# Attention and SwiGLU FFN on one core: joined score stretches, block-diagonal tails, and X^T of batches 1 to 7 by DMA transpose

## The chip, the cores and the metric

The kernel runs on one core of a Trainium2 chip. The metric is device time of one execution in microseconds; before the change it was 412.75 us (median of 3 runs, 411.9 to 414.39). Engine names below: PE is TensorE (matmul), PEld its weight loads, DVE VectorE, ACT ScalarE, POOL GpSimd, SP the engine that here only issues DMAs. Tile names in the profile lines: QKT (QK in the first two batches) the transposed Q and K, `st` or `s` the score tiles, PT their exponentials, VN the values of V, `X` or `f` the banks that value sums go to, XN the attention output, XS the same after normalizing, XT its transpose; WG, WV and WO are the FFN's gate, value and down weights, th and HT the steps between its up and down projections (HT also takes the first loads of q and k), ob the output.

## The reference

```python
# q, k, v: 8 batches, 8 heads, 576 positions, 64 wide
scores = q @ k.T / 8
mask   = (pos_i // 64) >= (pos_j // 64)          # blockwise causal
attn   = softmax(where(mask, scores, -1e9))
x      = (attn @ v)                               # 4608 tokens x 512
xn     = x / sqrt(mean(x*x) + 1e-6) * rms_g
out    = (silu(xn @ w_gate) * (xn @ w_val)) @ w_out    # 512 -> 1536 -> 512
```

## The kernel before

It works pair of heads by pair of heads ("slots", four per batch, 32 in all and four more at the end). A slot holds the score matmuls, exponentials and value matmuls of the attention; between these pieces a budgeted number of FFN steps from a queue is put in, four matmuls of 512 columns each, so that PE has work while ACT and DVE do the softmax. Matmuls write to PSUM, which the kernel divides into eight banks of 512 fp32 columns: two for scores, two for values, four for the FFN. It writes a bank again when the bank's last reader is done. The FFN of a batch can begin when its normalized X has been transposed ("X^T"). The parts that matter here:

```python
ST = ps.tile([P, 2 * BANK], FP32, name="st")                        # 2 PSUM banks: scores
XB = [ps.tile([P, BANK], FP32, name=f"X{i}") for i in range(2)]     # 2: values (and tails)
FB = [ps.tile([P, BANK], FP32, name=f"f{i}") for i in range(4)]     # 4: FFN, in rotation

def qk(self, dst, h, c, lo, w):              # head h: partitions 64h to 64h+63
    ds = slice(h * D, (h + 1) * D)
    mm(dst, KT[ds, k0:k0 + P], QT[ds, lo:lo + w])       # 64 rows, two heads side by side

# scores(n): the group's matmuls into ST, then one exponential of 1024 columns ST -> PT.
# In group 2 also the last 64 keys ("tail"), one matmul and one exponential per head,
# into the last 64 columns of XB[0] and XB[1]:
    self.qk(XB[h][:, BANK - BLK:BANK], h, NC, TAIL, BLK)
...
# norm_scale: XS = X / rms (bf16).  norm_transpose: per 128 columns, PE transposes into an
# FFN bank, ACT copies to X^T with the norm weight as per-partition scale.
    pe(nc.tensor.transpose(x[:, j*P:(j+1)*P], XS[:, j, p*P:(p+1)*P], ident))
    nc.scalar.activation(out=xt_tiles[i][:, p, ...], in_=x[:, ...], func=AF.Copy,
                         scale=gscale[:, p:p + 1])
...
# a slot: scores 0, values 0 (of the previous pair), scores 1, values 1, scores 2,
# with a fifth of the FFN budget after each
```

The softmax here doesn't subtract the row's maximum and nothing guards it: scores larger than these inputs give would overflow.

## Time and profile before

| | before |
|---|---|
| time, median | 412.75 us |
| PE busy | 379.6 us, 92% |
| DVE busy | 249.4 us, 61% |
| ACT busy | 235.5 us, 57% |
| score tile waits (PE st <- ACT PT) | 7.4 us |

The first part of the page gives each engine's busy time, share of the span and number of instructions.

```profile
span 412.1 us, 7988 instructions
PE 379.6 (92%) x3096; PEld 193.4 (47%) x3096; DVE 249.4 (61%) x652; ACT 235.5 (57%) x451; POOL 134.0 (33%) x184
```

Where PE is idle is seen in the windows view (columns: window, its length, then busy time and number of instructions of PE, PEld, DVE, ACT and POOL; granted PE clock; DMA share; GB/s).

```profile
0.00:30.00 30.00, 14.40 (x187) 9.13 (x188) 15.55 (x59) 10.96 (x18) 20.01 (x31) 1.00 1.29 163
90.00:120.00 30.00, 27.79 (x231) 13.18 (x227) 18.80 (x46) 18.98 (x38) 14.86 (x20) 1.00 0.94 93
120.00:160.00 40.00, 39.60 (x326) 19.04 (x323) 27.00 (x71) 25.96 (x49) 16.85 (x24) 1.00 0.92 98
160.00:200.00 40.00, 39.67 (x325) 19.05 (x324) 26.19 (x72) 25.97 (x52) 16.85 (x24) 1.00 0.89 101
```

From 120 us on PE is busy 99% of the time, until its last matmul, and ACT and DVE have a third of their time free. There, only a shorter PE stream can shorten the kernel. What each piece of that stream costs is read from start to start, not from the recorded durations, because matmuls overlap. Two cuts of the PE timeline (start, length, operation, count):

```profile
135.36 0.44 PE L346 MATMUL f_90<-ident,XS 128*128 128x128 bf16 x5
135.64 1.03 PE L87 MATMUL f_91<-WO,HT 128*128 128x512 bf16 x4
...
143.38 1.03 PE L87 MATMUL f_88<-XT,WG 128*128 128x512 bf16 x4
144.34 0.39 PE L87 MATMUL st<-QKT 64*128 64x448 bf16 x4
144.67 1.04 PE L87 MATMUL f_89<-XT,WV 128*128 128x512 bf16 x4
145.54 0.61 PE L87 MATMUL X_87<-VN_95,PT_96 128*128 128x65 bf16 x15
```

Four matmuls of 512 columns take 0.87 us to the start of what follows (144.67 to 145.54). In front of a score stretch it is 0.96 (143.38 to 144.34), and the stretch itself takes 0.33 where its columns, two heads at a time, need 0.22: some 0.2 us per stretch go into entering and leaving. Five transposes of X take 0.28 us, 56 ns each, though each is recorded with more than 200 ns. The Trainium skill, "TensorE: Matmul & The Clock Gate", Part 1, gives 55 to 56 ns between matmuls of 128 columns at full clock; this trace agrees. (Its Part 4 gives about 275 ns for a PE transpose in a kernel; inside this busy stream that is nearer to the recorded length, 226 ns on average, than to the cost.)

The clock column needs one correction. The trace's record of the clock begins at 33.5 us, and the view prints 1.00 for the time that has no record. For most of that time PE ran at half speed: value matmuls start 55 ns apart up to 33.4 us and 29 ns apart from 33.6 us, and up-projection matmuls of 256 columns 213 ns up to 32.2 us and 109 ns from 33.7 us.

In the early part PE waits. The longest lines of the list of waits (who waited for whom: total us, times, longest):

```profile
PE f_88 L178 <- DMA HT<-in_q_dram: 6.5, 2, 4.7
PE st L87 <- ACT PT_96 L246: 4.0, 5, 1.6
PE X_87 L87 <- DVE XN L284: 3.3, 4, 2.1
PE f_91 L87 <- ACT ob L408: 2.1, 6, 0.5
PE st L87 <- ACT PT_96 L249: 1.8, 2, 1.0
PE st L87 <- ACT PT_97 L246: 1.6, 2, 1.0
...
PE X_86 L87 <- DVE XN L284: 1.0, 1, 1.0
```

The `st` lines are scores that wait until the exponential has emptied the one score tile (7.4 us together), the `X` lines are tails that wait until the values have left their bank (4.3 us).

### The profile page before, as it was taken

The numbers are of one execution on the slowest core, as the hardware profiler recorded it, in microseconds if no ns is written. First come the engines' busy times: TensorE is split into PE (matmuls) and PEld (weight loads), VectorE is DVE, ScalarE is ACT, GpSimd is POOL, SyncE is SP. The second block draws the span as 40 slices with busy tenths as digits, with TensorE's granted clock in tenths as the row PEclk, the third lists the DMA queues.
The fourth block names the chain that finished last, engine by engine and source line by source line (L and its number), as shares of the span: only waits on it lengthen the run. The fifth ranks groups of instructions, "written<-read, shape, count | busy, mean of one in ns | idle before, by whom it ended". The sixth has DMA issues, their size and how long they took to land.

```text
span 412.1 us, 7988 instructions
## 1 busy us (share of the span) xinstructions
PE 379.6 (92%) x3096; PEld 193.4 (47%) x3096; DVE 249.4 (61%) x652; ACT 235.5 (57%) x451; POOL 134.0 (33%) x184
## 2 busy tenths in 40 slices
PE   3469779887999999999999999999999999999996
PEld 2337545664444544454445444544454444444442
DVE  5455864673779276926692669267926872752760
ACT  2276756786585758576757575757674625322321
POOL 8643497886079006910691060000000000000000
PEclk9999998999999999999999999999999999999999
DMA  9999999999299639972998397231020002002002
GB/s 99 190 203 186 169 89 169 131 149 130 61 107 117 105 76 102 110 128 68 83 125 130 70 79 69 86 81 35 0 78 27 0 27 76 1 2 102 1 2 102
DMA packets 140950, 36.70 MB, mean 89 GB/s; under 512 B 127600, under 2 KB 136304, under 8 KB 140912
## 3 DMA queue, kind: packets, MB, share of 16 engines
q0 software_dynamic: 103712, 18.89, 56.8%
q1 hardware_dynamic: 37200, 17.31, 18.4%
q8 instruction: 24, 0.39, 0.4%
q14 instruction: 14, 0.11, 0.1%
HBM read 37.75 MB, written 9.44 MB: 115 GB/s over the span
## 4 chain that ended last, share of the span: by engine, by line
PE 75%; DVE 12%; ACT 7%; DMA 2%; issue 2%; POOL 1%; ACTq 0%; POOLq 0%; DVEq 0%
PE f_91 L87 19%; PE f_89 L87 15%; PE f_88 L87 15%; PE f_90 L87 12%; PE st L87 6%; PE X_86 L87 3%; PE X_87 L87 3%; DVE HT L395 2%; DVE th L389 2%; DVE XS L333 2%; DMA HT<-in_k_dram 2%; ACT th L388 2%; DVE XN L284 2%; ACT sq L318 2%; ACT PT_96 L246 1%
## 5 line engine op out<-in xcount | busy, mean ns | idle before, releaser
L87 PEld LDWEIGHTS <-WV 128*128 128x128 bf16 x480 | 43.5, 98 | 45.9 <-issue 6.9
L87 PEld LDWEIGHTS <-WG 128*128 128x128 bf16 x480 | 43.5, 98 | 42.9 <-issue 4.3
L87 PEld LDWEIGHTS <-HT 128*128 128x128 bf16 x432 | 38.6, 98 | 47.3 <-issue 9.6
L389 DVE SCALAR_TENSOR_TENSOR th<-th,f_88 128x512 f32<-128x512 f32 x53 | 36.4, 686 | 40.3 <-ACT th L388 39.9
L87 PE MATMUL f_90<-XT,WG 128*128 128x512 bf16 (+1 forms) x248 | 56.7, 356 | 0.0
L87 PE MATMUL f_91<-XT,WV 128*128 128x512 bf16 (+1 forms) x240 | 55.7, 358 | 0.0
L87 PE MATMUL f_89<-XT,WV 128*128 128x512 bf16 (+1 forms) x240 | 55.7, 358 | 0.0
L87 PE MATMUL f_88<-XT,WG 128*128 128x512 bf16 (+1 forms) x232 | 55.4, 366 | 0.0
L388 ACT ACTIVATE th<-f_88 128x512 f32<-128x512 f32 x53 | 31.9, 603 | 40.3 <-PE f_88 L87 39.2
L246 ACT ACTIVATE PT_96<-st 128x1024 bf16<-128x1024 f32 x44 | 45.1, 1024 | 16.2 <-PE st L87 16.2
L246 ACT ACTIVATE PT_97<-st 128x1024 bf16<-128x1024 f32 x44 | 45.7, 1038 | 11.4 <-PE X_87 L87 6.6
L87 PE MATMUL f_91<-WO,HT 128*128 128x512 bf16 x192 | 48.2, 384 | 2.1 <-ACT ob L408 2.1
L389 DVE SCALAR_TENSOR_TENSOR th<-th,f_90 128x512 f32<-128x512 f32 x55 | 37.7, 686 | 19.0 <-ACT th L388 18.9
L388 ACT ACTIVATE th<-f_90 128x512 f32<-128x512 f32 x55 | 33.1, 601 | 27.6 <-PE f_90 L87 24.6
L395 DVE TENSOR_TENSOR HT<-th,f_89 128x512 bf16<-128x512 f32 x54 | 37.1, 687 | 5.6 <-PE f_89 L87 1.6
L395 DVE TENSOR_TENSOR HT<-th,f_91 128x512 bf16<-128x512 f32 x54 | 37.1, 686 | 3.6
L78 POOL DMA_DIRECT2D VN_95<-in_v_dram x20 | 17.1, 874 | 51.6 <-PE X_87 L87 45.7
L87 PE MATMUL st<-QKT 64*128 64x512 bf16 (+4 forms) x240 | 28.2, 297 | 2.2 <-ACT PT_97 L246 1.6
L78 POOL DMA_DIRECT2D VN_94<-in_v_dram x20 | 17.1, 906 | 36.6 <-PE X_87 L87 36.6
L87 PE MATMUL f_88<-WO,HT 128*128 128x512 bf16 x108 | 26.2, 380 | 0.2 <-DVE HT L395 0.2
L78 POOL DMA_DIRECT2D QKN_92<-in_k_dram x30 | 23.0, 766 | 8.9 <-DMA QKT<-QKN_92 3.4
L318 ACT ACTIVATE sq<-XN 128x512 bf16<-128x512 f32 x40 | 25.6, 639 | 0.1
(126 smaller groups left out, 475.5 us busy)
## 6 DMA issues: line engine op xcount, KB each, us to landing
out_dram<-ob SPq DMA_DIRECT2D x36, 256.0 KB, 2.0
VN_94<-in_v_dram POOLq DMA_DIRECT2D x16, 128.0 KB, 4.8
VN_95<-in_v_dram POOLq DMA_DIRECT2D x16, 128.0 KB, 4.7
WG<-in_moe_w_gate_dram POOLq DMA_DIRECT2D x4, 384.0 KB, 10.8
WV<-in_moe_w_val_dram POOLq DMA_DIRECT2D x4, 384.0 KB, 11.7
WO<-in_moe_w_out_dram POOLq DMA_DIRECT2D x2, 768.0 KB, 14.0
QKN_92<-in_k_dram POOLq DMA_DIRECT2D x24, 64.0 KB, 3.5
QKN_92<-in_q_dram POOLq DMA_DIRECT2D x24, 64.0 KB, 3.6
```

The source lines that it names most:

```text
L78: return chain("POOL", nc.gpsimd.dma_start(**kw))
L87: pe(nc.tensor.matmul(dst, w, r, start=start, stop=stop))
L246: nc.scalar.activation(out=PT[:, a0:a0 + T4], in_=ST, func=AF.Exp, scale=SM_SCALE)
L284: nc.vector.tensor_tensor(out=xn_tiles[self.b][:, t0:t0 + n, f0:f0 + m * D].rearrange("p t (h d) -> p h t d", h=m), in0=xv[:, :, :, 0:D], ...
L318: nc.scalar.activation(out=sq, in_=XN[:, t, :], func=AF.Square, accum_out=ss[:, j:j + 1])
L333: nc.vector.tensor_scalar(out=XS[:, j, :], in0=XN[:, t, :], scalar1=rs[:, j:j + 1], scalar2=None, op0=ALU.mult)
L388: nc.scalar.activation(out=th, in_=pg, func=AF.Tanh, scale=0.5)
L389: nc.vector.scalar_tensor_tensor(out=th, in0=th, scalar=1.0, in1=pg, op0=ALU.add, op1=ALU.mult)
L395: nc.vector.tensor_tensor(out=ht, in0=gates.pop((i, k)), in1=pv, op=ALU.mult)
```

## The change

Three things at once. Score stretches: a second score tile, and two score groups one after the other, so that two slots have three stretches in place of six. Tails: the last 64 keys of both heads lie block-diagonally in one 128 x 128 K tile, so one 128-row matmul and one exponential do both heads. X^T of batches 1 to 7: root and norm weight are applied in one DVE operation, and DMA transposes issued from SP write X^T, with no PE transpose and no ACT copy. The second score tile takes the two X banks; values and tails now rotate through the four FFN banks.

```diff
-    ST = ps.tile([P, 2 * BANK], FP32, name="st")
-    XB = [ps.tile([P, BANK], FP32, name=f"X{i}") for i in range(2)]
+    ST = [ps.tile([P, T4], FP32, name=f"s{i}") for i in range(2)]
     FB = [ps.tile([P, BANK], FP32, name=f"f{i}") for i in range(4)]
+    def fbank(hold=None):                 # the oldest bank that no down sum holds
+        ...
+        def tail(self):
+            x = fbank()[:, 0:BLK]
+            mm(x, KT, QT[:, TAIL:S])      # KT block-diagonal: both heads, 128 rows
 ... norm_scale ...
+            nc.vector.scalar_tensor_tensor(out=XS[:, j, :], in0=XN[:, t, :],
+                                           scalar=rs[:, j:j + 1], in1=grow,
+                                           op0=ALU.mult, op1=ALU.mult)
+            ...   # for each FFN chunk that this tile touches
+                    sp(nc.sync.dma_start_transpose(out=xt(i)[:, :, lo - a:hi - a],
+                                                   in_=XS[lo - g0:hi - g0, j, :]))
 ... slots ...
-        at(norms, s1, lambda b=b, tiles=tiles: xt_by_pe(b, tiles))
+        if b == 0:
+            at(norms, s1, lambda b=b, tiles=tiles: xt_by_pe(b, tiles))
+        elif s % 2 == 0:
+            pieces = [lambda: session((cur, 0), (cur, 1))] + val + [None]
+        else:
+            pieces = [lambda: session((prev, 2), (cur, 0)), val[0],
+                      lambda: session((cur, 1), (cur, 2)), val[1], None]
 ... V and K tails loaded to match, PT cleared whole, norm weight row loaded at the start,
 ... one more QKT buffer, two more output buffers
```

More of the change, by code (lines that the diff above doesn't have):

```diff
@@ L47 @@
     TAIL = NC * P
-    PTW = 6 * BANK + 5 * BLK
+    T4 = 2 * BANK
+    PTT = 3 * T4
+    PTW = PTT + P + 3 * BLK
     const = ctx.enter_context(tc.tile_pool(name="const", bufs=1))
-    tp = ctx.enter_context(tc.tile_pool(name="tp", bufs=3))
+    tp = ctx.enter_context(tc.tile_pool(name="tp", bufs=4))
     xtp = ctx.enter_context(tc.tile_pool(name="xtp", bufs=3))
@@ L57 @@
     hbuf = ctx.enter_context(tc.tile_pool(name="hbuf", bufs=3))
-    obuf = ctx.enter_context(tc.tile_pool(name="obuf", bufs=2))
+    obuf = ctx.enter_context(tc.tile_pool(name="obuf", bufs=4))
     ps = ctx.enter_context(tc.tile_pool(name="ps", bufs=1, space=bass.MemoryType.PSUM))
@@ L87, in mm, with stbank @@
         pe(nc.tensor.matmul(dst, w, r, start=start, stop=stop))
-    ST = ps.tile([P, 2 * BANK], FP32, name="st")
-    XB = [ps.tile([P, BANK], FP32, name=f"X{i}") for i in range(2)]
+    ST = [ps.tile([P, T4], FP32, name=f"s{i}") for i in range(2)]
     FB = [ps.tile([P, BANK], FP32, name=f"f{i}") for i in range(4)]
+    held = set()
+    order = list(range(4))
     turn = [0]
-    def fbank():
+    def fbank(hold=None):
+        i = next(i for i in order if i not in held)
+        order.remove(i)
+        order.append(i)
+        if hold is not None:
+            held.add(i)
+            hold.append(i)
+        return FB[i]
+    def stbank():
         turn[0] += 1
-        return FB[(turn[0] - 1) % 4]
+        return ST[(turn[0] - 1) % 2]
     QKN = [const.tile([P, HP, 2 * NQT, P], BF16, name=f"QKN{i}") for i in range(2)]
@@ L100 @@
     PTS = [const.tile([P, PTW], BF16, name=f"PT{i}") for i in range(2)]
+    KB = const.tile([P, 2 * HP, P], BF16, name="KB")
     QK0 = [const.tile([P, 2, S], BF16, name=f"QK0{i}") for i in range(2 * HP)]
@@ L103 @@
     gscale = const.tile([P, HP], FP32, name="gscale")
+    grow = const.tile([P, DM], FP32, name="grow")
     WG = const.tile([P, HP, DFF], BF16, name="WG")
@@ L120, in load_v_tail @@
     def load_v_tail(b):
-        pool_dma(out=VN[b % 2][BLK:P, NC, :, 0:D],
-                            in_=v[b, :, TAIL:S, :].rearrange("h p d -> p h d"))
+        for par in range(2):
+            pool_dma(out=VN[b % 2][par * BLK:(par + 1) * BLK, NC, par:H:2, 0:D],
+                     in_=v[b, par:H:2, TAIL:S, :].rearrange("h p d -> p h d"))
     def load_v_chunk(b, c):
@@ L143, in load_qk_tail @@
             pool_dma(
-                out=t[0:BLK, :, NQT + NC, ds],
+                out=t[ds, :, NQT + NC, ds],
                 in_=k[b, par:H:2, TAIL:S, :].rearrange("h p d -> p h d"))
@@ L160, in clear_v @@
     def clear_v(i):
-        nc.vector.memset(VN[i][:, 0:NC, :, D:VP], 1.0)
-        nc.vector.memset(VN[i][0:BLK, NC, :, :], 0.0)
-        nc.vector.memset(VN[i][BLK:P, NC, :, D:VP], 1.0)
+        nc.vector.memset(VN[i][:, :, :, D:VP], 1.0)
+        for par in range(2):
+            nc.vector.memset(VN[i][(1 - par) * BLK:(2 - par) * BLK, NC, par:H:2, :], 0.0)
     def clear_qkn(i):
-        for n in range(2):
-            nc.vector.memset(QKN[i][BLK:P, :, n * NQT + NC, :], 0.0)
+        nc.vector.memset(QKN[i][BLK:P, :, NC, :], 0.0)
+        for par in range(2):
+            nc.vector.memset(QKN[i][par * BLK:(par + 1) * BLK, :, NQT + NC,
+                                    (1 - par) * BLK:(2 - par) * BLK], 0.0)
     tposed = {}
@@ L182, in tpose_wide @@
                                   in_=t[:, 0:S].rearrange("p (s j) -> p j s", s=SLOT))
-        tposed[b, hp] = T[:, 0, :], T[:, 1, :]
+        KT = KB[:, b * HP + hp, :]
+        for par in range(2):
+            ds = slice(par * D, (par + 1) * D)
+            nc.vector.tensor_copy(out=KT[ds, ds], in_=T[ds, 1, TAIL:S])
+        tposed[b, hp] = T[:, 0, :], T[:, 1, :], KT
     def prep(b, hp):
@@ L187, in prep @@
         sp(nc.sync.dma_start_transpose(out=T, in_=QKN[b % 2][:, hp, :, :]))
-        tposed[b, hp] = [T[:, n * NQT:(n + 1) * NQT, :].rearrange("p c q -> p (c q)")
-                         for n in range(2)]
-    T4 = 2 * BANK
-    LAST = (NC, TAIL, BLK)
+        q_, k_ = [T[:, n * NQT:(n + 1) * NQT, :].rearrange("p c q -> p (c q)")
+                  for n in range(2)]
+        tposed[b, hp] = q_, k_, k_[:, NC * P:NQT * P]
     FULL = ([[(0, 0, 512, 0)], [(1, 128, 448, 0), (0, TAIL, BLK, 448)],
@@ L197 @@
     EARLY = ([[(0, 0, 256, 0), (1, 128, 128, 256)]], [(0, 0, 256, 4)], range(0, 2))
-    LATE = ([[(0, 256, 320, 0), (3, 384, 192, 320)], [(1, 256, 320, 0), (NC, TAIL, BLK, 320)],
+    LATE = ([[(0, 256, 320, 0), (3, 384, 192, 320)], [(1, 256, 320, 0)],
              [(2, 256, 320, 0)]],
@@ L212, in __init__ @@
             self.base = T4 * (k // 2) if plan is EARLY else 0
-            self.bank = k % 2
-            self.col = {}
+            self.col, self.todo = {}, {}
             if plan is not LATE and hp == 0:
                 xn_tiles[b] = xp.tile([P, NQT, DM], FP32, name="XN")
-        def qk(self, dst, h, c, lo, w):
-            QT, KT = tposed[self.b, self.hp]
-            ds = slice(h * D, (h + 1) * D)
-            k0 = min(c * P, S - P)
-            mm(dst, KT[ds, k0:k0 + P], QT[ds, lo:lo + w])
@@ L224, in scores @@
-        def scores(self, n, split=None):
-            st = split or [ST[:, h * BANK:(h + 1) * BANK] for h in range(2)]
+        def scores(self, n):
+            QT, KT, _ = tposed[self.b, self.hp]
+            st = stbank()
+            a0 = self.base + n * T4
+            end = 0
+            for c, lo, w, o in self.groups[n]:
+                for h in range(2):
+                    ds = slice(h * D, (h + 1) * D)
+                    mm(st[:, h * BANK + o:h * BANK + o + w], KT[ds, c * P:(c + 1) * P],
+                       QT[ds, lo:lo + w])
+                    for t in range(NQT):
+                        if lo <= t * P < lo + w:
+                            self.col[h, c, t] = a0 + h * BANK + o + t * P - lo
+                end = max(end, o + w)
+            self.todo[n] = st, end
@@ L226, in scores, with exps @@
+        def exps(self, n):
+            st, end = self.todo.pop(n)
             PT = self.PT
             a0 = self.base + n * T4
-            end = 0
-            tail = self.full and n == 2
-            for c, lo, w, o in self.groups[n]:
-                for h in range(2):
-                    self.qk(st[h][:, o:o + w], h, c, lo, w)
-                    for t in range(NQT):
-                        if lo <= t * P < lo + w and (c < NC or t == NC):
-                            self.col[h, c, t] = a0 + h * BANK + o + t * P - lo
-                end = max(end, o + w)
@@ L237, in scores @@
-            if tail:
-                for h in range(2):
-                    self.qk(XB[h][:, BANK - BLK:BANK], h, NC, TAIL, BLK)
-                    self.col[h, NC, NC] = 3 * T4 + h * BLK
-            if split:
-                for h in range(2):
-                    nc.scalar.activation(out=PT[:, a0 + h * BANK:a0 + h * BANK + end],
-                                         in_=st[h][:, 0:end], func=AF.Exp, scale=SM_SCALE)
-            elif end == BANK:
-                nc.scalar.activation(out=PT[:, a0:a0 + T4], in_=ST, func=AF.Exp,
-                                     scale=SM_SCALE)
+            if end == BANK:
+                nc.scalar.activation(out=PT[:, a0:a0 + T4], in_=st, func=AF.Exp, scale=SM_SCALE)
@@ L250, in scores @@
                     out=PT[:, a0:a0 + T4].rearrange("p (h q) -> p h q", h=2)[:, :, 0:end],
-                    in_=ST.rearrange("p (h q) -> p h q", h=2)[:, :, 0:end],
+                    in_=st.rearrange("p (h q) -> p h q", h=2)[:, :, 0:end],
                     func=AF.Exp, scale=SM_SCALE)
-            if tail:
-                for h in range(2):
-                    a = 3 * T4 + h * BLK
-                    nc.scalar.activation(out=PT[:, a:a + BLK], in_=XB[h][:, BANK - BLK:BANK],
-                                         func=AF.Exp, scale=SM_SCALE)
             for tn, o, step, cnt in self.diags:
@@ L262, in scores, with both, tail_exp @@
                     nc.vector.memset(blk[:, :, 0:BLK], 0.0)
+        def both(self, n):
+            self.scores(n)
+            self.exps(n)
+        def tail(self):
+            QT, _, KT = tposed[self.b, self.hp]
+            x = fbank()[:, 0:BLK]
+            mm(x, KT, QT[:, TAIL:S])
+            self.todo[3] = x
+        def tail_exp(self):
+            x = self.todo.pop(3)
+            nc.scalar.activation(out=self.PT[:, PTT:PTT + BLK], in_=x, func=AF.Exp,
+                                 scale=SM_SCALE)
+            for h in range(2):
+                self.col[h, NC, NC] = PTT
         def values(self, part):
@@ L269, in values @@
             t0 = self.qts[0]
-            bank = part if self.full else self.bank
-            X = XB[bank][:, 0:len(heads) * n * VP]
+            X = fbank()[:, 0:len(heads) * n * VP]
             for i, h in enumerate(heads):
@@ L332, in one @@
             rs = norm_tiles[b, tiles[0], "rs"]
-            nc.vector.tensor_scalar(out=XS[:, j, :], in0=XN[:, t, :],
-                                    scalar1=rs[:, j:j + 1], scalar2=None, op0=ALU.mult)
+            if b == 0:
+                nc.vector.tensor_scalar(out=XS[:, j, :], in0=XN[:, t, :],
+                                        scalar1=rs[:, j:j + 1], scalar2=None, op0=ALU.mult)
+                return
+            nc.vector.scalar_tensor_tensor(out=XS[:, j, :], in0=XN[:, t, :],
+                                           scalar=rs[:, j:j + 1], in1=grow,
+                                           op0=ALU.mult, op1=ALU.mult)
+            g0 = b * S + t * P
+            g1 = b * S + min(S, (t + 1) * P)
+            for i, (a, e) in enumerate(chunks):
+                lo, hi = max(a, g0), min(e, g1)
+                if lo < hi:
+                    sp(nc.sync.dma_start_transpose(out=xt(i)[:, :, lo - a:hi - a],
+                                                   in_=XS[lo - g0:hi - g0, j, :]))
         return [root] + [lambda j=j, t=t: one(j, t) for j, t in enumerate(tiles)]
@@ L339, with xt @@
     xt_tiles = {}
+    def xt(i):
+        if i not in xt_tiles:
+            xt_tiles[i] = xtp.tile([P, HP, chunks[i][1] - chunks[i][0]], BF16, name="XT")
+        return xt_tiles[i]
     def norm_transpose(b, tiles, p):
@@ L350, in norm_transpose @@
             if lo < hi:
-                if i not in xt_tiles:
-                    xt_tiles[i] = xtp.tile([P, HP, e - a], BF16, name="XT")
-                nc.scalar.activation(out=xt_tiles[i][:, p, lo - a:hi - a],
+                nc.scalar.activation(out=xt(i)[:, p, lo - a:hi - a],
                                      in_=x[:, lo - g0:hi - g0],
@@ L401, in down @@
         if part == 0:
-            outs[i, s] = fbank()
-        po = outs[i, s]
+            outs[i, s] = []
+            fbank(outs[i, s])
+        po = FB[outs[i, s][0]]
         for m in range(part * 4, part * 4 + 4):
@@ L408, in down @@
             nc.scalar.mul(out=ob, in_=po, mul=0.5)
+            held.discard(outs[i, s][0])
             r0 = chunks[i][0] + s * P
@@ L444 @@
     sp(nc.sync.dma_start(out=gscale, in_=moe_rms_g.rearrange("(c p) -> p c", p=P)))
+    sp(nc.sync.dma_start(out=grow, in_=moe_rms_g.rearrange("(o f) -> o f", o=1).to_broadcast([P, DM])))
     clear_v(0)
     for t in PTS:
-        for o in (1408, 1920, 2368, 2880, 3200):
-            nc.vector.memset(t[:, o:o + BLK], 0.0)
+        nc.vector.memset(t, 0.0)
+    for par in range(2):
+        nc.vector.memset(KB[par * D:(par + 1) * D, :, (1 - par) * D:(2 - par) * D], 0.0)
     T0, T1, TA = [0, 1], [2, 3, 4], [0, 1, 2, 3, 4]
@@ L465 @@
         tpose_wide(0, hp)
-        early[hp].scores(0, (None, FB[0:2], FB[2:4])[hp % 3])
+        early[hp].both(0)
         if hp > 1:
@@ L496 @@
         s1 = s0 + (1 if fast else 2)
-        at(norms, s1, lambda b=b, tiles=tiles: xt_by_pe(b, tiles))
+        if b == 0:
+            at(norms, s1, lambda b=b, tiles=tiles: xt_by_pe(b, tiles))
         at(rels, s1, lambda b=b, tiles=tiles: release(b, tiles))
@@ L530, with session, end3 @@
             cur = Pair(sl[0], sl[1], LATE if sl[0] == 0 else FULL)
-        pieces = []
-        for n in range(3):
-            pieces.append((lambda n=n: cur.scores(n)) if cur else None)
-            if n < 2:
-                pieces.append((lambda n=n: prev.values(n)) if prev else None)
+        val = [(lambda n=n: prev.values(n)) if prev else None for n in range(2)]
+        bo = [(lambda n=n: cur.both(n)) if cur else None for n in range(3)]
+        def session(*groups):
+            for p_, n in groups:
+                p_.scores(n)
+            for p_, n in groups:
+                if n == 2:
+                    p_.tail()
+            for p_, n in groups:
+                p_.exps(n)
+                if n == 2:
+                    p_.tail_exp()
+        if not cur:
+            pieces = val + [None, None, None]
+        elif not cur.full:
+            def end3():
+                cur.tail()
+                cur.both(2)
+                cur.tail_exp()
+            pieces = [bo[0], val[0], bo[1], val[1], end3]
+        elif s % 2 == 0:
[3 more added lines that the diff above has]
+                      lambda: session((cur, 1), (cur, 2)), val[1], None]
         if s == e0:
             tpose_wide(1, 0)
-            pieces = [pieces[1], pieces[3], pieces[0], pieces[2], pieces[4]]
+            pieces = [val[0], pieces[0], None, None]
+        shares = [1.0] * len(pieces)
         left = 0
@@ L544 @@
                 mids[s]()
-            if i == 3 and s > e0:
+            if i == len(pieces) - 2 and s != e0:
                 aside.extend(todo)
                 todo = []
-            if i >= 3 and todo:
+            if i >= len(pieces) - 2 and todo:
                 todo.pop(0)()
-            left = ffn(left + budget / len(pieces))
+            left = ffn(left + budget * shares[i] / sum(shares))
         for f in todo + aside + rels.pop(s, []) + pp + loads.pop(s, []):
```

## The prediction

> **What bounds the kernel now.** TensorE. The page gives PE 379.6 of 412.1 us (92%); the chain that ended last is 75% PE. In the windows view, 120 to 320 us has PE busy 39.6 of every 40 us, ACT about 26, DVE about 25. Idle PE time lies mostly before 95 us and in the last 4 us. So in the steady part only PE's own instruction stream counts; before 95 us the waits do.
>
> **What the change takes off PE.**
> 1. 140 of 160 XS transposes. The records say 226 ns each, but on the timeline they start 56 ns apart: 140 x 0.056 = 7.9 us.
> 2. Score stretches. The score matmuls use 64 rows, two heads side by side; the Trainium skill, "TensorEngine Tiling (Array Packing)", Key Properties, says that changing the tiling mode drains the array. The timeline agrees: matmuls of up-projections start 216 ns apart, a score after one 312 ns, and leaving costs about 100 ns again: 0.20 us per stretch. The 28 full pairs go from 84 stretches to 42: 8.4 us.
> 3. Tails. Two 64-row matmuls into the value banks become one 128-row matmul; in the steady part the second starts on average 78 ns late: about 2 us.
> 4. Early waits, 45 to 96 us: scores wait for the single score tile (PE st <- ACT exp, about 4.5 us), tails for XN to leave X_86/X_87 (4.3 us). Two score tiles, and tails outside the value banks, should remove 5 to 6 us.
> Sum: about 24 us.
>
> **Off PE.** ACT loses 56 X^T copies (about 0.55 us, 31 us) and 24 tail exponentials (0.23 us, 5.5 us). DVE: 35 XS operations become scalar_tensor_tensor, 622 to about 690 ns, +2 us. SP gains 39 DMA transposes; QKT ones, 2.5 times larger, land in 4.8 us, and X^T is wanted a slot (about 10 us) later, so I expect no wait.
>
> **What it adds to PE.** The second score tile takes the two X banks, so values and tails share the four FFN banks, and a down sum holds one. A joined stretch puts two exponentials (1.03 us each), sometimes a tail's, in front of the next tanh (0.60) and its DVE product (0.69). A gate bank written after a stretch comes free about 4.1 us after the stretch began; its next user wants it at 3.8: 0.2 to 0.5 us at many of the 42 stretches, two thirds of which stand among up-projections: +6 us. At the start two whole-tile memsets (64x264 uint32 took 0.28 us, so about 1.8 us each, an estimate) delay the first DVE copy by some 0.3 us.
>
> **Prediction.** 412.75 - 24 + 6 = about 395 us. Range 386 to 404. Faster by over 2%: 0.90; within 2%: 0.09; slower: 0.01.
>
> **What would show it.** PE busy falls by 15 to 22 us; XS transposes 20; score entries about half as many. ACT falls to about 200 us. In the list of waits "PE st <- ACT PT" and "PE X <- DVE XN" nearly vanish; new "PE f <- DVE th, HT or XN" and "PE f <- ACT" lines of 3 to 10 us. What 120 to 320 us of before does shrinks by 6 to 8 us, the first 120 us by about 6. No PE wait on X^T's DMA.
>
> **What would make it wrong.** Bank waits above 10 us (then 400 or more); X^T transposes queued behind QKT ones or loads while the DMA engines are full (before 175 us), so that FFN work starves; or banks that cost nothing and early waits that go wholly (then 387).

## The result, and the profile after

The changed kernel takes 401.22 us (median of 4 runs, 397.96 to 401.96) against 413.27 us before in the same rounds. The ratio is 0.969, 95% interval 0.964 to 0.974. Ratios here and below are the mean time of one kernel's runs over that of the other's of the same rounds, so not quite the ratio of the medians. Executions over 1.5% slower than the fastest of the same kernel are left out of the means. The gain, 12 us, is two thirds of the predicted 18.

```profile
span 399.9 us, 7708 instructions
PE 367.2 (92%) x2924; PEld 187.5 (47%) x2924; DVE 259.3 (65%) x664; ACT 208.7 (52%) x369; POOL 138.0 (35%) x192
```

PE lost 172 matmuls, ACT 27 us. The windows:

```profile
0.00:30.00 30.00, 13.96 (x184) 8.85 (x185) 20.64 (x64) 10.53 (x18) 20.48 (x32) 1.00 1.29 171
90.00:120.00 30.00, 26.17 (x199) 11.97 (x196) 18.87 (x45) 14.66 (x26) 14.06 (x20) 0.94 1.16 125
120.00:160.00 40.00, 39.54 (x321) 19.14 (x318) 27.59 (x75) 24.39 (x44) 19.43 (x27) 1.00 1.20 120
160.00:200.00 40.00, 39.46 (x317) 19.00 (x314) 27.47 (x73) 24.40 (x46) 19.44 (x27) 1.00 1.13 120
```

PE is as full as before from 120 us on, so what its stream saves there is saved time. The timeline shows a joined stretch: the eight matmuls of two groups in one go (the line names the shape of the first), then the one tail matmul, which costs 40 ns.

```profile
141.38 1.03 PE L89 MATMUL f<-XT,WG 128*128 128x512 bf16 x4
142.34 0.61 PE L89 MATMUL s<-QKT 64*128 64x448 bf16 x8
142.88 0.20 PE L89 MATMUL f<-QKT 128*128 128x64 bf16 x1
142.92 1.03 PE L89 MATMUL f<-XT,WV 128*128 128x512 bf16 x4
143.79 0.61 PE L89 MATMUL f<-VN,PT 128*128 128x65 bf16 x15
```

Entering takes 0.96 in place of 0.87 again, and the eight matmuls take 0.54 where their columns need 0.43: the same 0.2 us, for two groups. Counted over the trace, a score matmul follows something else 56 times, before 95 times.

The list of waits has changed its names, not its sum (the waits for QK, 4.3 us, were 3.8 before, in four smaller lines):

```profile
PE f L195 <- DMA HT<-in_q_dram: 6.6, 1, 6.6
PE s L89 <- DVE QK L198: 4.3, 4, 1.3
PE f L89 <- DVE PT L268: 4.0, 4, 1.3
PE f L89 <- DVE th L426: 2.6, 7, 0.6
PE f L89 <- DMA XT<-XS: 2.3, 1, 2.3
PE s L89 <- ACT PT L258: 1.7, 2, 1.0
PE f L89 <- DVE XN L306: 1.5, 1, 1.5
```

To separate the two parts of the kernel, a mark that both programs pass is needed. The start of the 65th of the 432 matmuls of the down projection serves: it lies near 133 us, in batch 3 of the attention (counted from 0), and the work from there to the start of the last matmul is the same in every version but for what the change takes away. Idle time in front of PE matmuls, summed on each side of the mark, and the time at half PE clock that the trace records before the mark, without the start (all in us):

| kernel (its profiled run) | mark at | idle before mark | half clock before mark | mark to last matmul | idle after mark |
|---|---|---|---|---|---|
| before | 133.2 | 26.1 | 3.4 | 274.7 | 2.6 |
| changed | 132.9 | 26.8 | 6.8 | 262.8 | 2.1 |

So in these two runs the gain lies after the mark: 11.9 us there, 0.3 us before it. The part before the mark varies from run to run: a second profile of the changed kernel (`after_again` below) has its mark at 130.7, so 0.3 to 2.5 us are gained there against the one profile of before. The change also takes work from PE before the mark (20 transposes and 13 of the 39 stretches, about 3.7 us at the costs above). Of that, 0.2 to 0.7 us went to more idle time. The clock took another part: the changed kernel has 3.4 us more of half clock, and full clock was first granted at 35.7 us in the one run and 33.0 in the other, against 33.5 before. At half speed this costs up to 2.8 and 1.5 us, an estimate from these lengths.

### The profile page after: what moved, and what is told of

Same layout as the page of the kernel before. It is cut to its first block, busy times and chain, and to the rows that moved or that the text cites. A ratio compares the mean times of both kernels' runs of the same rounds, so it can differ in the third digit from the quotient of the medians.

```text
span 399.9 us, 7708 instructions
## 1 busy us (share of the span) xinstructions
PE 367.2 (92%) x2924; PEld 187.5 (47%) x2924; DVE 259.3 (65%) x664; ACT 208.7 (52%) x369; POOL 138.0 (35%) x192
## 4 chain that ended last, share of the span: by engine, by line
PE 70%; DVE 12%; ACT 11%; issue 3%; DMA 3%; POOL 1%; DVEq 0%; POOLq 0%; ACTq 0%
PE f L89 65%; ACT sq L340 5%; PE s L89 4%; ACT PT L258 3%; DVE th L426 2%; ACT th L425 2%; DVE HT L432 2%; DMA HT<-in_k_dram 2%; DVE QK L198 2%; DVE XN L306 1%; DMA XT<-XS 1%; DVE XS L356 1%; POOL HT L80 1%; DVE PT L268 1%; DVE y L320 1%
## 5 line engine op out<-in xcount | busy, mean ns | idle before, releaser
L89 PE MATMUL f<-XT,WG 128*128 128x512 bf16 (+1 forms) x480 | 112.9, 363 | 3.7 <-DMA XT<-XS 2.3
L89 PE MATMUL f<-XT,WV 128*128 128x512 bf16 (+1 forms) x480 | 113.2, 364 | 0.0
L425 ACT ACTIVATE th<-f 128x512 f32<-128x512 f32 x108 | 64.2, 596 | 84.2 <-PE f L89 76.4
L426 DVE SCALAR_TENSOR_TENSOR th<-th,f 128x512 f32<-128x512 f32 x108 | 74.0, 685 | 52.0 <-ACT th L425 51.2
L89 PE MATMUL f<-WO,HT 128*128 128x512 bf16 x432 | 99.7, 379 | 1.8 <-DVE XN L306 1.5
L258 ACT ACTIVATE PT<-s 128x1024 bf16<-128x1024 f32 x88 | 86.9, 1023 | 10.8 <-PE s L89 10.7
L432 DVE TENSOR_TENSOR HT<-th,f 128x512 bf16<-128x512 f32 x108 | 74.1, 686 | 8.8 <-PE f L89 1.8
L80 POOL DMA_DIRECT2D QKN<-in_q_dram x60 | 49.0, 816 | 5.0 <-DMA WO<-in_moe_w_out_dram 3.4
L80 POOL DMA_DIRECT2D QKN<-in_k_dram x60 | 48.7, 812 | 5.1 <-DMA WO<-in_moe_w_out_dram 2.1
L89 PE MATMUL f<-VN,PT 128*128 128x65 bf16 x960 | 44.1, 198 | 4.8 <-DVE PT L268 4.0
```

The lines of the kernel that those rows point to most:

```text
L80: return chain("POOL", nc.gpsimd.dma_start(**kw))
L89: pe(nc.tensor.matmul(dst, w, r, start=start, stop=stop))
L258: nc.scalar.activation(out=PT[:, a0:a0 + T4], in_=st, func=AF.Exp, scale=SM_SCALE)
L425: nc.scalar.activation(out=th, in_=pg, func=AF.Tanh, scale=0.5)
L426: nc.vector.scalar_tensor_tensor(out=th, in0=th, scalar=1.0, in1=pg, op0=ALU.add, op1=ALU.mult)
L432: nc.vector.tensor_tensor(out=ht, in0=gates.pop((i, k)), in1=pv, op=ALU.mult)
```

## The experiments

Each ran five rounds against the kernel before. Those of one group (the anchor, xt_by_pe, unjoined and b1_by_pe; neither, act_back, grow_late and b1_early; the last three of the table; tails_two by itself) shared a chip and its runs of before. The mark table of all of them:

| kernel | ratio to before, 95% interval | mark at | idle before | half clock before | mark to end | idle after |
|---|---|---|---|---|---|---|
| changed, again | 0.9657 (0.9626 to 0.9688) | 130.7 | 26.3 | 6.8 | 262.8 | 2.1 |
| xt_by_pe | 0.9779 (0.9741 to 0.9817) | 134.7 | 25.8 | 13.7 | 269.7 | 2.2 |
| unjoined | 0.9846 (0.980 to 0.9891) | 135.2 | 26.2 | 13.7 | 267.5 | 2.9 |
| tails_two | 0.9904 (0.9866 to 0.9941) | 130.2 | 26.8 | 3.4 | 271.2 | 8.5 |
| neither | 1.0025 (0.9983 to 1.0068) | 131.0 | 25.8 | 0.0 | 279.0 | 6.8 |
| act_back | 0.9647 (0.961 to 0.9684) | 133.1 | 27.5 | 6.8 | 262.6 | 2.1 |
| grow_late | 0.9652 (0.9621 to 0.9683) | 130.2 | 27.6 | 3.4 | 262.8 | 2.1 |
| b1_by_pe | 0.9623 (0.9592 to 0.9653) | 130.0 | 25.0 | 3.4 | 262.9 | 2.1 |
| b1_early | 0.9807 (0.9779 to 0.9835) | 137.6 | 31.7 | 13.7 | 262.8 | 2.1 |
| b1_early_prep3 | 0.9633 (0.9602 to 0.9663) | 130.0 | 25.6 | 6.8 | 262.8 | 2.1 |
| b1_pe_unjoin89 | 0.9607 (0.9573 to 0.964) | 128.8 | 23.5 | 3.4 | 262.9 | 2.1 |
| b1_early_all | 0.9636 (0.9597 to 0.9676) | 129.0 | 26.1 | 3.4 | 263.1 | 2.3 |

The theory: the steady part gained what PE's own stream lost, and in the early part the waits only moved. The rivals are in the expectations.

**The anchor.** The changed kernel, once more.

> The changed kernel as it is, once more, as the anchor of this group. Both theories: 0.969 of before, about 400.5 us; in the profile PE waits about 2.3 us for the DMA of X^T near 100 us (if that wait belongs to the kernel and not to one run).

It held: the median is 400.44 us, and the wait for X^T near 100 us is there again with 2.2 us.

**X^T by PE again.**

```diff
-            if b == 0:
+            if True:                     # XS by tensor_scalar, no DMA transpose
-        if b == 0:
+        if True:
             at(norms, s1, lambda b=b, tiles=tiles: xt_by_pe(b, tiles))
```

> X^T of all batches by TensorE again, everything else as changed. Theory A (the gain is TensorE's own stream: 140 transposes started 56 ns apart = 7.8 us, less what the DMA way loses near 100 us: 2.3 us of waiting and about 1.7 us at half clock): +4 us against the changed kernel. Rival B (the gain of this part is the 31 us of ScalarE copies that go away): +8 us or more, and new PE waits for ACT. Rival C (the DMA way costs nothing early): +8 us with waits as before.

The ratio is 0.0122 above that of the changed kernel, about 5.1 us of 414.5. After the mark it is 269.7 against 262.8: 6.9 us for 120 transposes, 57 ns each, with idle time unchanged. The profiled run of this kernel was its slowest (410.3, the others 404.5 to 407.6) and had more half-clock time than the rest, so its early numbers are not typical; the part after the mark is free of that. Theory A fits.

**ScalarE put back.** Theory A and rival B differ on whether ACT's relief had a share.

```diff
+                    nc.scalar.activation(out=dum[:, 0:hi - lo], in_=flat[:, lo - g0:hi - g0],
+                                         func=AF.Copy, scale=gscale[:, p:p + 1])
```

> The changed kernel with the 56 ScalarE copies of X^T put back as dead work of the same widths (into a tile that nobody reads), about 31 us of ScalarE. Theory A (ScalarE had slack, the gain of X^T by DMA is TensorE's 56 ns per transpose): within 1.5 us of the changed kernel. Rival B (ScalarE relief is the gain): +4 us or more.

0.9647 against 0.9657 (from another call): no difference, and 262.6 against 262.8 us after the mark. ACT's time was not worth anything. (ACT was busy 235.1 us again, as before the change. The copies put back read XS and not PSUM, so the run does not give back the PSUM banks that the old copies emptied.)

**Stretches unjoined.**

```diff
-        elif s % 2 == 0:
-            pieces = [lambda: session((cur, 0), (cur, 1))] + val + [None]
-        else:
-            pieces = [lambda: session((prev, 2), (cur, 0)), ...]
+        else:
+            pieces = [bo[0], val[0], bo[1], val[1], end3]      # as in the first batch
```

> Every pair has its three score stretches of its own again (84 instead of 42), two score tiles, block-diagonal tails and X^T by DMA as changed. Theory A (each stretch costs 0.20 us of drain): +8.4 us in the steady part, less the waits that the joined stretches bring (values waiting for exp and mask, bank waits, about 3 us early): +5 to +8 us. Rival B (stretches overlap with weight loads and cost nothing): within 2 us.

The cost is 0.0189, about 7.8 us. After the mark there are 52 stretches in place of 26, and 4.7 us more: 0.18 us for each. Of the 4.7 us, 0.8 are idle time. Rival B is out. With the 6.9 us of the transposes this makes 11.6 of the 11.9 us that the whole change gained after the mark. The rest of the 7.8 us is early, where this kernel's runs also divide by clock: 405.3 and 405.6 us at a mean granted clock of 0.994 and 0.996, 408.7 to 409.9 at 0.982.

**Tails undone.**

```diff
-            x = fbank()[:, 0:BLK]
-            mm(x, KT, QT[:, TAIL:S])
+            x = [fbank()[:, 0:BLK] for h in range(2)]
+            for h in range(2):
+                mm(x[h], KT[ds, :], QT[ds, TAIL:S])            # 64 rows; two exponentials
 ... V, Q and K tails loaded and cleared as in the kernel before
```

> The changed kernel with the tails undone: two 64-row matmuls per pair into two of the four shared banks, two exponentials, V and K tails laid out as before; joined stretches and X^T by DMA stay. Theory A (in the steady part a tail's second matmul no longer waits for XN, so only about 30 to 80 ns per pair are at stake, against one more bank taken): after the 65th down matmul +0 to +2 us, in all 0 to +3 us. Rival B (the tails are a main part of the gain, or the bank they save is): +4 us or more.

My theory missed, and rival B came true: 0.9904 against 0.9657, some 10 us. After the mark it is 8.4 us, of which 6.4 are new idle time (8.5 against 2.1). The list of waits says whose:

```profile
PE f L89 <- ACT PT L279: 7.9, 18, 0.8
...
PE f L89 <- DVE HT L428: 3.3, 7, 0.6
PE f L89 <- DVE th L422: 2.4, 3, 1.3
```

L279 is the tail's exponential. In a joined stretch it stands behind one or two exponentials of 1.02 us; until it has run, the tail's bank is taken, and with two tails two of four rotating banks are.

```profile
181.22 0.61 PE L89 MATMUL s<-QKT 64*128 64x448 bf16 x8
181.66 0.19 PE L89 MATMUL f<-QKT 64*128 64x64 bf16 x2
181.79 1.04 PE L89 MATMUL f<-XT,WV 128*128 128x512 bf16 x4
182.69 0.61 PE L89 MATMUL f<-VN,PT 128*128 128x65 bf16 x15
183.92 1.02 PE L89 MATMUL f<-XT,WG 128*128 128x512 bf16 x4 [0.62 <-ACT PT L279]
```

Two tails, one up-projection and the values fill the four banks; the next gate matmul wants the first tail's, starts 2.26 us after the tails, and has waited 0.62 us. It is the bank and not the second exponential that it waits for: the first tail's exponential ended at 183.87 us, the matmul started at 183.92, and the second ended only at 183.99. Of the 8.4 us, 2.0 remain for the matmul itself, 0.11 us for each of the 18 pairs after the mark. So in this layout the block-diagonal tail is worth little as a shorter matmul, and much as a saved bank: it is what makes room for the second score tile.

**Neither joined stretches nor DMA transposes.** What is left is the second score tile, the shared banks and the tails.

> Stretches unjoined and X^T of all batches by TensorE: what is left of the change is the second score tile, values and tails in the shared banks, and the block-diagonal tail. Theory A (early waits only moved: the waits that the second score tile removes come back as waits for the mask, the XN copy and the DVE products): 0.985 to 1.0 of before; score-tile waits near zero, sum of PE waits before 135 us again about 25 us. Rival B (the early waits go, as I predicted): 0.98 or less. If the parts add up: 400.3 + 5.1 + 7.8 = 413 us against 414.5.

1.0025: no gain at all. (One of its six runs was slow and is left out.) Theory A's range ended at 1.0, so this is just outside it; the parts do not add up, 413 us was the sum and 415.9 is the median of the five runs. After the mark it is 16.2 us slower than the changed kernel, where the two steps alone cost 6.9 and 4.7; the rest is mostly idle time (6.8 against 2.1). Against the kernel before it is 4.3 us slower there, with 6.8 us idle against 2.6. Its longest new line, PE transposes that wait for an output copy to free their bank, is 5.9 us in 7 waits, where `xt_by_pe` has 0.8. Before the mark the score-tile waits are down to 1.6 us, as the second tile should do, and yet the idle sum is 25.8 us. That is the step of my prediction that failed, seen on its own.

**The norm weight row later.** At the start, the first q load was in use at 4.70 us before and at 6.64 after.

```diff
-    sp(nc.sync.dma_start(out=grow, in_=moe_rms_g....to_broadcast([P, DM])))
+    pool_dma(out=grow, ...)              # behind load_down_weights
```

> The 256 KB load of the norm weight row is put behind the weights in the POOL queue in place of the very start. Theory A (it competes with the first q and k loads, whose first use moved from 4.7 to 6.6 us): the first transpose starts near 4.7 us again. Whether time falls: up to -1.5 us if the DMA of the first 14 us is the limit throughout, 0 if the later loads of q and k set the pace anyway, as the two traces agree again at 12.2 us.

The first wait is 4.7 us again, so the 256 KB row does delay the first load. The time is the same (0.9652): idle time up to the last value matmul of the first two query tiles is 14.7 us there, 12.6 in the changed kernel. The wait moved to a later load of q (2.8 us at 14.3 us); why that one landed later, no run shows.

**Why is X^T of batch 1 late?** In the changed kernel, on SP, DVE and PE:

```profile
90.50 3.40 DVE L359 SCALAR_TENSOR_TENSOR XS<-XN,y,grow 128x512 bf16<-128x512 f32 x5
...
91.28 7.70 SPq L367 DMA_TRANSPOSE XT<-XS  x6
...
96.76 1.03 PE L89 MATMUL f<-WO,HT 128*128 128x512 bf16 x4
...
100.13 1.48 PE L89 MATMUL f<-XT,WG 128*128 128x512 bf16 x4 [2.34 <-DMA XT<-XS]
```

DVE has all five tiles scaled at 93.9 us. SP is busy 1.2 us with each transpose (39 of them: 1.18 to 2.42, median 1.21 us), no less for a half tile of 64 rows, and starts one each 1.3 us. The fourth, the last one that the waiting chunk needs, is issued at 95.19 and lands 4.8 us later, at 100.0. Then PE stands 2.34 us, and a stretch of 3.4 us at half clock follows, which costs up to 1.7. The Trainium skill, "TensorE: Matmul & The Clock Gate", Part 1, says that the clock falls to half after at least one idle window of about 3.4 us, on a free-running grid. The traces agree on the grid: before the mark such stretches last 3.41, 6.83 or 10.24 us and begin whole multiples of 3.41 us after full clock was first granted, and none lies between 106 us and the end. They do not agree that the window must be idle throughout: in the 3.4 us in front of this one PE waited 2.3 us, in front of the one at 83.5 us of the same trace 1.7 us. Cut by this grid, the 14 traces have 21 windows before the mark that a half-clock stretch follows, with 1.2 to 2.5 us of waiting in each. Every window at full clock with 1.85 us or more was followed by one; windows with 1.2 to 1.7 us sometimes were and sometimes not. Two ways to take the lateness away:

```diff
-            if b == 0:                   # (twice)
+            if b < 2:                    # batch 1 by PE too
```

> X^T of batch 1 by TensorE as of batch 0, batches 2 to 7 by DMA. Theory A (the X^T of batch 1 comes too late because the DMA transposes take some 9 us from the first XS to the last landing, and TensorE idles 2.3 us and then runs 3.4 us at half clock): 20 transposes cost 1.1 us, the wait and the slow stretch go, in all -2 to -3 us. Rival B (the work runs out there whatever the way): 0 to +1 us, with a wait for XS or for a PSUM bank in its place.

```diff
-        at(norms, s0 + (0 if fast else 1), lambda ...: norm_scale(b, tiles))
+        at(norms, s0 + (0 if b < 2 else 1), lambda ...: norm_scale(b, tiles))
```

> The XS operations and DMA transposes of batch 1 are issued one slot earlier, its FFN chunks released where they were. Theory A (the DMA way is late, not the work): the wait for X^T near 100 us vanishes and the slow-clock stretch after it too, -2 to -4 us, without TensorE transposes. Rival B (the squares and the XN copies are not ready earlier, so nothing moves): 0, the wait stays at 2 us.

With PE for batch 1 the wait for the DMA is gone and the ratio is 0.0034 lower, 1.4 us. The intervals of the ratios overlap, but both contain the noise of the same runs of before. The two kernels ran in the same rounds, so they can be compared directly: five of the six runs (398.23 to 399.07 us, the sixth 400.13) lie below all six of the anchor (399.43 to 400.99). So the gain is shown, though it is less than the 2 to 3 us expected. Waits for XS, 2.9 in place of 1.0 us, took part of it. The other way was a miss: 0.9807, 6 us slower. Its longest wait is a new one:

```profile
88.91 7.98 SPq L367 DMA_TRANSPOSE XT<-XS  x6
...
97.06 2.95 SPq L208 DMA_TRANSPOSE QKT<-QKN  x2
...
100.62 0.61 PE L89 MATMUL s<-QKT 64*128 64x512 bf16 x2 [7.20 <-DMA QKT<-QKN]
```

SP issued in program order. The Q and K transpose of slot 11 stood behind six X^T transposes and the DVE work that these wait for (SP had waited 17.8 us for the first scaled tile). If that is the cause, issuing the Q and K transposes of batch 2 a slot sooner must repair it:

```diff
+        at(preps, index[b, hp] - (3 if b == WIDE else 2), ...)    # and tp bufs=5
```

> As b1_early, but the Q and K transposes of batch 2 are issued three slots ahead (a fifth buffer), so none of them stands behind the X^T transposes of batch 1 in the SP queue. Theory (b1_early lost because the SP queue is served in order and the QKT of slot 11 stood 8 us behind six X^T transposes): the 7.2 us wait for QKT goes, X^T is in time, 0.955 to 0.965 of before. Rival (XS is ready too late for either order, the queue order does not matter): the time stays near 0.98.

It did: 0.9633, no wait for QKT left, X^T's wait 1.4 us. The late issue in the queue was the whole loss. (The fifth buffer that the earlier issue needs came with it; no run has it alone.) Against the changed kernel the gain is no larger than the intervals.

**Less joining where the FFN queue is short.** In slots 8 and 9 a joined stretch has little FFN work behind it while its two exponentials run.

```diff
-        elif not cur.full:
+        elif not cur.full or s in (8, 9):
```

> X^T of batch 1 by TensorE, and slots 8 and 9 (the first two pairs of batch 2, where the FFN queue is short) keep three stretches of their own; all other slots joined. Theory (a joined stretch needs FFN work behind it while its two exponentials run; in slot 9 there is too little, 2.5 us of waiting): waits between the last value of batch 1 and the end of pair 1 of batch 2 fall from 2.7 us to about 1.5, three more stretches cost 0.5 us: about -0.7 us against b1_by_pe. Rival (waits only move): 0.

> b1_early_prep3 with slots 8 and 9 unjoined: X^T of batches 1 to 7 by DMA, no late X^T, no joined stretch where the FFN queue is short. If both theories hold it is the best of all: 0.955 to 0.96 of before, 396 to 398 us. If not, it lies between its two parents.

The first is the fastest kernel: 397.99 us, 0.9607 of before. Idle time before the mark falls to 23.5 us. Between the last value of batch 1 and the end of pair 1 of batch 2 the waits went from 2.7 to 2.0 us, less than expected. The second, which should have been the best, does no better than `b1_early_prep3` (0.9636 against 0.9633): its X^T wait is 2.1 us. PE comes to the end of pair 1 of batch 2 at 86.8 us there, in `b1_early_prep3` at 90.5, so perhaps it only arrives sooner at the same wait; no run shows that apart. Both beat the kernel before; over the changed kernel the first is ahead by some 2 us, on another chip, with overlapping intervals.

## Why the prediction was right or wrong

The time, 401.2 us, lies in the range (386 to 404), and "faster by over 2%" came true. The forecast gain of 18 us was 12. That it came out this near is in part luck: two terms that did not come, 5 to 6 us of early waits and 6 us of bank waits, had opposite signs.

- **Transposes, 56 ns each: right.** 57 ns after the mark (`xt_by_pe`), and ACT's relief worth nothing (`act_back`).
- **0.20 us per score stretch: right.** 0.18 us per stretch after the mark, idle time included (`unjoined`). The drain at a change of tiling mode, for which the prediction cites the skill, would explain such a cost; the runs show the cost and not the drain itself.
- **Tails, about 2 us: right for the matmul, but the larger part was left out.** I costed the second matmul's delay. Undoing the tail costs 8.4 us after the mark: 2.0 in PE's stream, and 6.4 of idle time because of the bank.
- **"Two score tiles, and tails outside the value banks, should remove 5 to 6 us" of early waits: this step failed.** The named waits did shrink: score tile from 7.4 to 2.5 us, XN from 4.3 to 2.5. But in their place stand values that wait for the mask of an exponential just issued (DVE PT, 0.8 to 4.0 us), X^T's DMA (0 to 2.3) and DVE products (0 to 1.2 before 135 us). Idle time before the mark is 26.1 us before and 26.8 after, and 25.0 to 27.6 in nine of the eleven other versions. About half of it, 12.3 and 12.6 us, lies before 21 us, where q and k are loaded. That no one wait sets the rest, but a chain of attention steps with too little FFN work to put between them, is what these sums suggest; it is not shown by a run that takes the chain away.
- **Bank waits, +6 us: the term was too large.** Idle time after the mark did not rise (2.6 to 2.1 us). The new waits of FFN matmuls for DVE products (th and HT) are 2.9 us in the whole kernel, 1.7 of them after the mark, and waits for output copies fell there from 2.1 us to none. With one more bank taken per tail (`tails_two`) the idle time was 8.5 us, so the margin was thin.
- **"No PE wait on X^T's DMA": wrong** for batch 1. I compared the transfer's landing time with a slot's length, and left out that SP spends 1.2 us on each of six transposes in turn. The half-clock stretch after it was not in the sum.
- **Signs.** XS transposes 20, stretches 56 in place of 95, ACT 208.7 us: as said. PE busy fell by 12.4 us, under the 15 to 22 named; the clock before the mark accounts for up to 2.8 us of what is missing. The XS operation took 745 ns, not 690.

In sum: of the 24 us, about 13 were forecast after the mark, and 11.9 came. The other 11 were forecast early: 5 to 6 as waits, which only moved, the rest as PE work, of which idle time and clock took so much that 0.3 to 2.5 us came. The 6 us of bank waits, taken off the 24, did not come either.

## What to carry to other kernels

Cost an engine's stream start to start, and trust such a sum only in the stretch where that engine is never idle; where several engines wait for one another by turns, removing one wait can give it to the next in line, as it did here. Count PSUM banks as part of a change's price or worth: here a merged pair of small matmuls was worth 8 us, and 6 of them because of the bank it freed. Work moved to a DMA queue is late by the issue time of everything in front of it, so place each issue by when its neighbours in the queue are wanted, as well as by its own deadline.

## What the Trainium skill lacked or had wrong

- "TensorEngine Tiling (Array Packing)", Key Properties: the drain at a change of tiling mode has no figure. Here entering and leaving a 64-row stretch cost 0.20 us together on the timeline, 0.18 us measured by undoing 26 joins.
- "TensorE: Matmul & The Clock Gate", Part 4: it gives about 275 ns for a PE transpose of 128 x 128 bf16 in a kernel, which is not what one costs in a full stream. Here 120 of them cost 6.9 us, 57 ns each.
- The same page, Part 1: half clock after an idle window of about 3.4 us. Here 21 half-clock stretches in 14 traces came after windows of that length in which PE waited 1.2 to 2.5 us; all windows with 1.85 us or more of waiting were followed by one. So a window need not be idle throughout, and a phase of short waits can cost up to 1.7 us more for each stretch of 3.4 us.
- "DMA: Bandwidth & Descriptors", DMA Transpose (X-bar): the section does not say what a transpose costs the issuing engine (elsewhere the page has sequencer cycles for other shapes, in a comparison with trn3, and none for this one). Here SP was busy 1.21 us (median of 39) with one of 128 x 512 bf16, as long with one of 64 rows, and a transpose that waited on DVE held back the later ones: a 7.2 us wait of PE for QKT.
- No page gives the time of a scalar_tensor_tensor with an added fp32 row against tensor_scalar at 128 x 512, fp32 to bf16 (one has a remark on its throughput, without a time): 745 against 622 ns here.
